# A filter table loaded earlier, a weight converted by its transfers, and finer steps beside the first two chunks of a fused FFT mixing and MLP kernel

## The chip, the cores and the metric

The kernel runs on one core of a Trainium2 chip. The metric is the device time of one execution in microseconds (us); lower is better. Of the engines, PE is the matrix engine (TensorE; PEld its weight loads), DVE the vector engine, ACT the scalar engine, POOL GpSimd and SP the engine that only issues transfers. Each engine works through its own instructions in order and waits where one of them is not ready. Transfers (DMA) run on 16 engines that all queues share; POOL and SP feed two different queues of them.

## The reference

```python
# x: 8 x 3008 x 256; filt_r, filt_i: 1505 x 256
X = rfft(x, axis=1)
y = irfft(X * (filt_r + 1j * filt_i)[None], n=3008, axis=1)
t = y.reshape(24064, 256)
# w_in: 256 x 2048, w_out: 2048 x 256, alpha: 2048
h = t @ w_in
s = sin(alpha * h)
out = (h + s * s / (alpha + 1e-9)) @ w_out
```

All inputs and the output are fp32. The kernel computes in fp16 with fp32 sums.

## The kernel before, in words

**The transform.** The length 3008 is split into 47 x 64. For one batch of 3008 rows, a first stage (`f1`, or `f1_chip` for batch 0) multiplies by a table of roots of order 47 (`wa`), a second (`f2x`) by `wb`, which gives the spectrum in `xs`; `product` multiplies it by the filter `fri` on DVE into `z` and `t2`; `f2g` (batch 0: `g_chip`) goes back by `wg` (and `wgs`), and `f3` by `we` into `yt`, which is the MLP's input. Between the stages the data must change its layout. Batches 1 to 7 do that through DRAM: `asb` is stored to `scr1` and read back as `bint` (`shuffle1`), `gsb` is stored to `scr2` and read back as `gin` (`shuffle2`); all of these go through SP's queue. Batch 0 does it on the chip, by multiplications with an identity: `turn1` ahead of `f2x`, `turn2` ahead of `f3`.

**The MLP.** The 24,064 rows are worked in 47 chunks `g` of 512 rows, each in 8 slots `q`. `mlp_in` multiplies by a block of `w_in16` and ACT takes the sine into `vt`; after every odd slot DVE squares four blocks (`square`); `mlp_out` of the chunk before multiplies `vt` by `w_out2` (`w_out` divided by `alpha`), and `yt` by `m_t`, the product of `w_in` and `w_out`, so that `h` itself is never kept. `evict_out` copies the sums `po` to `ot` on DVE, and `store_out` stores them by SP.

**The order.** Nothing schedules itself: the order in the program is the order on each engine. The part up to the first chunk is a written list. After that a dictionary `plan` says which work stands in which slot: `at(slot, f, ...)` puts it between the two `mlp_in` of that slot, and the loop calls it there. For batch 1, `f1` is put three to a slot from slot 5 on, `shuffle1` in slot 10, and the second stage from slot 14 on. Slots 0 to 13 (chunk 0, which has no `mlp_out` beside it, and most of chunk 1) also hold what is left over from the start: `turn2` 4 to 15, `prep_w_inT` (a transposed `w_in` for `m_t`), `prep_w_out` (`w_out2`), `prep_m` in slot 13, and `negate_filter`.

**Banks.** The matrix engine writes to eight banks: three `psf` (transform stages and preparations), three `psh` (`mlp_in`, `turn1`, `keep_busy`, half of `g_chip`) and two `pso` (`po` of `mlp_out`; before that, half of `g_chip`). A tile of a pool waits until the tile that had its bank has been evicted by ACT or DVE.

**Transfers at the start.** POOL issues `x` of batch 0 in four parts of two transfers each, then the filter in three parts (each of `filt_r` and `filt_i`, each in two transfers), then `w_in16`, all converted from fp32 to fp16 by the transfer. SP issues the tables; `gate(a, b)` makes the issue of transfer `a` wait until `b` has landed. The first third of `wb` goes at once; the rest waits for the first filter transfer, and the three slices of `wg` and `wgs` follow. `w_out` comes as fp32, its first half by SP behind a gate on `w_in16`, the second by POOL in slot 7; POOL converts each half to `w_out16` (`cast_w_out`). `load_x(1, 4)` brings batch 1's rows by POOL in eight transfers; it can start only when `f2x` of batch 0 is done with `bint`, whose memory it takes. `keep_busy` multiplies zeros, to no use but PE's clock.

Of the kernel before, what the change touches and what calls it, by code (L numbers as in the profile page):

```python
# [10 lines left out]
FP32 = mybir.dt.float32  # L11
# [53 lines left out]
def kernel(  # L65
# [57 lines left out]
    def gate(ins, earlier):  # L123

        tc.add_manual_dep(ins.ins, earlier.ins.name, mybir.DependencyInfo(
            mybir.DependencyClass.Sync, mybir.DependencyReason.DATA), reason="order of transfers")

    def load_x(b, parts=2):

        xt[b] = (xbpool if b else vpool).tile([GT, RP, C], FP16, name="xt", tag="xb" if b else "vt")  # L130
        n = RP // parts
        for h in range(parts):
            for p0, p1 in ((0, 80), (80, GT)):
                x_dma[b, h] = nc.gpsimd.dma_start(  # L134
                    out=xt[b][p0:p1, n * h:n * h + n, :],
                    in_=dram(x, (b * S + RP * p0 + n * h) * C, [[RP * C, p1 - p0], [1, n * C]]))
# [45 lines left out]

    def turn2(j):

        ps = psf.tile([4 * NK, 2, C], FP32, name="pst2", tag="f")
        rows = b_c.rearrange("p h r s a -> p h r (s a)")
        for i in range(2):
            for half in range(2):
                nc.tensor.matmul(out=ps[:, i, 128 * half:128 * half + 128],
                                 lhsT=rows[:, half, 2 * j + i], rhs=ident, start=True, stop=True)  # L190
        (nc.scalar.copy if j in (0, 2, 12, 14) else nc.vector.tensor_copy)(  # L191
            out=gin[0][:, 2 * j:2 * j + 2, :], in_=ps)

    def shuffle1(b):
# [88 lines left out]
    def mlp_out(g, q, h):  # L283

        if q == h:
            po[g, h] = pso.tile([128, 2, C], FP32, name="po", tag="po")
        if not 0 <= q - h < 7:
            return
        for n in range((q - h) * 36 // 7, (q - h + 1) * 36 // 7):
            k, i = divmod(n, 2)  # L290
            t = 2 * h + i
            ts = slice(128 * t, 128 * t + 128)
            nc.tensor.matmul(out=po[g, h][:, i, :],  # L293
                             lhsT=vt[g][:, k, ts] if k < 16 else yt[g][:, k - 16, t],
                             rhs=w_out2[:, k, :] if k < 16 else m_t[:, k - 16, :],
                             start=(n == 0), stop=(n == 35))
# [38 lines left out]
    alpha_r = cpool.tile([16, 128], FP32, name="alpha_r")  # L335
    alpha_t = cpool.tile([128, 16], FP32, name="alpha_t")
    recip = cpool.tile([128, 16], FP32, name="recip")
    w_inT, w_out32, w_in32, alpha_b = [], [], [], []

    def prep_alpha():  # L340
        ps = pso.tile([128, 2, C], FP32, name="psal", tag="po")
# [2 lines left out]
        nc.vector.tensor_scalar(out=recip, in0=alpha_t, scalar1=1e-9, scalar2=None, op0=ALU.add)  # L344
        nc.vector.reciprocal(out=recip, in_=recip)

    def load_w_out(h, eng):
        w_out32.append(stpool.tile([128, 8, C], FP32, name="w_out32", tag="st"))
        return eng.dma_start(out=w_out32[h],
                             in_=moe_w_out[1024 * h:1024 * h + 1024, :].rearrange("(b p) c -> p b c", p=128))  # L350

    def cast_w_out(h):
        nc.gpsimd.tensor_copy(out=w_out16[:, 8 * h:8 * h + 8, :], in_=w_out32[h])

    def prep_w_out(h, k):
        for i in range(4 * k, 4 * k + 4):
            nc.vector.tensor_scalar(out=w_out2[:, 8 * h + i, :], in0=w_out32[h][:, i, :],
                                    scalar1=recip[:, 8 * h + i:8 * h + i + 1], scalar2=None,
                                    op0=ALU.mult)

    def prep_w_inT(k):
        if k == 0:
            w_inT.append(ginpool.tile([128, 16, C], FP16, name="w_inT", tag="gin"))
        ps = psf.tile([128, 2, C], FP32, name="pst", tag="f")
        for i in range(2):
            for cb in range(2):
                jb = 2 * k + i
                nc.tensor.matmul(out=ps[:, i, 128 * cb:128 * cb + 128],
                                 lhsT=w_in16[:, cb, 128 * jb:128 * jb + 128],
                                 rhs=ident, start=True, stop=True)  # L370
        (nc.scalar.copy if k % 2 else nc.vector.tensor_copy)(
            out=w_inT[0][:, 2 * k:2 * k + 2, :], in_=ps)
# [45 lines left out]
    plan = {}  # L418

    def at(slot, f, *args):  # L420
        plan.setdefault(int(slot), []).append((f, args))

    for b in range(1, B):
        p = MT * (b - 1)
        u0, un, x0, step = (5, 3, 14, 1.1) if b == 1 else (p - 9, 2, p + 4, 1.9)
        for u in range(16):
            at(u0 + u // un, f1, b, u)
        at(u0 + 16 // un, shuffle1, b)
        for k in range(6):
            xa, xb = x0 + int(2 * k * step), x0 + int((2 * k + 1) * step)  # L430
            at(xa, f2x, b, 2 * k)
            at(xb, f2x, b, 2 * k + 1)
            at(xb + 1, product, b, k, 0)
            at(xb + 2, product, b, k, 1)
            at(xb + 4, f2g, b, 2 * k)
            at(xb + 5, f2g, b, 2 * k + 1)
        at(xb + 6, shuffle2, b)
        if b + 1 < B:
            at(xb + 1, load_x, b + 1)
    G = 2  # L440
    for g in range(NCH - 1):
        todo = []
        while G < 8 * B and GT * G < 128 * (g + 2):
            todo += [(G, 0), (G, 1)]
            G += 1
        slots = (4, 6) if len(todo) == 2 else (3, 4, 6, 7) if g == 4 else (3, 4, 5, 6)
        for q, u in zip(slots, todo):
            at(8 * g + q, f3, *u)
    for k in range(2):
        at(6 + k, prep_w_out, 0, k)  # L450
        at(10 + k, prep_w_out, 1, k)
        at(13, prep_m, k)
    at(6, cast_w_out, 0)
    at(7, load_w_out, 1, nc.gpsimd)
    at(10, cast_w_out, 1)
    at(14, load_w_in32, 0)
    at(22, load_w_in32, 1)
    for k in range(8):
        at(5 + k, prep_w_inT, k)
        at(18 + k + 3 * (k // 4), prep_w_ina, k // 4, k % 4)  # L460

    for k in range(3):
        at(11 + k, negate_filter, 8 * k, 8)
    for j in range(4, 16):
        at((j - 4) * 5 // 12, turn2, j)

    with tc.manual_schedule():
        nc.sync.dma_start(out=wa2, in_=wa2_d.ap())
# [18 lines left out]
                w_in_dma[h, cb] = nc.gpsimd.dma_start(out=w_in16[:, cb, hs],  # L487
                                                      in_=moe_w_in[128 * cb:128 * cb + 128, hs])
        wgs = ginpool.tile([128, NK * 128], FP16, name="wgs", tag="gin")
        gate(nc.sync.dma_start(out=wb[:, 8 * 128:], in_=wb_d.ap()[:, 8 * 128:]), filter_dma[0, 0])  # L490
        for s0 in (0, 8, 16):
            cs = slice(128 * s0, 128 * s0 + 1024)
            ins = nc.sync.dma_start(out=wg[:, cs], in_=wg_d.ap()[:, cs])
            if s0:
                gate(ins, filter_dma[s0, 0])
            nc.sync.dma_start(out=wgs[:, cs], in_=wgs_d.ap()[:, cs])
        a_c = vpool.tile([128, 2, NK, 128], FP16, name="a_c", tag="vt")
        prep_alpha()
# [7 lines left out]
        for f, *args in (  # L506
                (turn1, 0), (turn1, 1), (turn1, 2), (f2x, 0, 0), (turn1, 3), (turn1, 4), (f2x, 0, 1),
                (turn1, 5), (turn1, 6), (f2x, 0, 2), (turn1, 7), (fold_filter, 0, 8), (turn1, 8),
                (f2x, 0, 3), (product, 0, 0, 0), (turn1, 9), (f2x, 0, 4), (turn1, 10), (f2x, 0, 5),
                (product, 0, 1, 0), (turn1, 11), (keep_busy, 2, zero), (f2x, 0, 6), (f2x, 0, 7), (g_chip, 0, 0), (g_chip, 0, 1),  # L510
                (fold_filter, 8, 8), (f2x, 0, 8), (keep_busy, 2, zero), (product, 0, 2, 0), (g_chip, 1, 0), (g_chip, 1, 1),
                (f2x, 0, 9), (keep_busy, 2, zero), (product, 0, 3, 0), (f2x, 0, 10), (f2x, 0, 11), (keep_busy, 2, zero), (g_chip, 2, 0), (g_chip, 2, 1),
                (fold_filter, 16, 8), (keep_busy, 2, zero), (product, 0, 4, 0), (g_chip, 3, 0), (g_chip, 3, 1),
                (product, 0, 5, 0), (keep_busy, 2, zero), (g_chip, 4, 0), (g_chip, 4, 1), (keep_busy, 2, zero), (g_chip, 5, 0), (g_chip, 5, 1),
                (keep_busy, 1, zero)):
            f(*args)
        gin[0] = ginpool.tile([4 * NK, RP, C], FP16, name="gin", tag="gin")
        for j in range(4):
            turn2(j)
        gate(load_w_out(0, nc.sync), w_in_dma[0, 1])  # L520
        load_x(1, 4)
        for i in range(4):
            if i % 2 == 0:
                keep_busy(1, zero)
            f3(i // 2, i % 2)

        for g in range(NCH):
            for q in range(8):
                if g and q == 7:
                    evict_out(g - 1, 0)  # L530
                mlp_in(g, 2 * q)
                if g:
                    mlp_out(g - 1, q, 1)
                for f, args in plan.get(8 * g + q, ()):
                    f(*args)
                mlp_in(g, 2 * q + 1)
                if g:
                    mlp_out(g - 1, q, 0)
                if g and q == 7:
                    evict_out(g - 1, 1)  # L540
                    store_out(g - 1, 0, 4, (nc.sync,))
                if q % 2:
                    square(g, q)
# [29 lines left out]
```

## Time and profile before

| | |
|---|---|
| three runs, median | 836.46 us (836.37 to 837.84) |
| the profiled execution, its own time | 836.65 us |
| its span, first to last instruction | 834.9 us |
| busy: PE | 815.2 us (98%), 6242 matmuls |
| busy: ACT, DVE, POOL | 619.4, 513.4, 37.5 us |
| mean granted PE clock | 0.998 |
| first `mlp_in`; `prep_m`; first `mlp_in` of chunk 4 | 38.0, 70.7, 115.3 us |

Times in the profile are us from the start of the span. "Busy" is the time in which an engine has an instruction at work, and matmuls overlap: the distance between two starts says what a matmul really takes. A line such as `PE a L204 <- DMA b: 3.6, 1, 3.6` says that PE stood idle before line 204 of the kernel for 3.6 us in total, once, 3.6 at the longest, until the transfer of `b` had landed.

### The profile page before, as it was taken

What the parts mean: (1) busy time and instruction counts of PE and PEld (TensorE: products, weight loads), DVE (VectorE), ACT (ScalarE), POOL (GpSimd) and SP (SyncE); (2) the same over time, 40 slices, a digit from 0 to 9 for tenths busy, and PEclk for the clock granted to TensorE, in tenths of its full rate; (3) what the DMA queues carried; (4) which work ended last, traced back from release to release, by engine and by line L of the source; (5) the groups of instructions that cost most, each with busy time, mean ns of one, the idle gap of its engine ahead of it and who ended that gap; (6) DMA issues with size and microseconds to landing.
All of it is one profiled execution on the core that took longest, in us unless ns stands there. A gap on an engine that the chain in (4) does not pass through costs nothing.

```text
span 834.9 us, 15135 instructions
## 1 busy us (share of the span) xinstructions
PE 815.2 (98%) x6242; PEld 572.4 (69%) x6242; DVE 513.4 (61%) x676; ACT 619.4 (74%) x1155; POOL 37.5 (4%) x66
## 2 busy tenths in 40 slices
PE   6979999999999999999999999999999999999997
PEld 3647676777667776677767776677766777767666
DVE  4788966676466665576655684567655675443442
ACT  4786987787777877788777887778877787666663
POOL 6211000000000000000000000000000000000000
PEclk9999999999999999999999999999999999999999
DMA  9926383424543163612834146331645123210111
GB/s 196 246 85 244 105 205 84 144 73 113 139 110 119 51 162 89 202 40 65 193 95 139 51 110 168 102 101 51 168 110 150 53 101 92 62 51 26 26 52 51
DMA packets 67061, 92.33 MB, mean 111 GB/s; under 512 B 5512, under 2 KB 51352, under 8 KB 65480
## 3 DMA queue, kind: packets, MB, share of 16 engines
q1 hardware_dynamic: 60704, 72.04, 30.1%
q0 software_dynamic: 5760, 19.14, 11.0%
q8 instruction: 49, 0.80, 0.4%
q10 hardware_dynamic: 528, 0.18, 0.1%
q14 instruction: 20, 0.16, 0.1%
HBM read 59.62 MB, written 46.66 MB: 127 GB/s over the span
## 4 chain that ended last, share of the span: by engine, by line
PE 91%; DVE 3%; DMA 3%; issue 2%; POOL 0%; ACT 0%; POOLq 0%
PE po L293 42%; PE ph L274 37%; PE psa L143 2%; PE psy L262 2%; PE psx L204 2%; PE psg L234 2%; DMA w_out<-in_moe_w_out_dram 1%; PE pe L307 1%; DMA wb<-wb_tbl 1%; DMA xt<-in_x_dram 1%; PE psg L177 1%; DVE vt L281 1%; DVE gin L191 1%; DMA fri<-in_filt_r_dram 0%; PE idle L397 0%
## 5 line engine op out<-in xcount | busy, mean ns | idle before, releaser
L276 ACT ACTIVATE vt<-ph 128x512 f16<-128x512 f32 x688 | 404.8, 602 | 142.1 <-PE ph L274 137.2
L293 PE MATMUL po<-w_out,vt 128*128 128x256 f16 x2944 | 426.6, 272 | 1.3 <-DVE ot L318 0.8
L293 PEld LDWEIGHTS <-vt 128*128 128x128 f16 x2944 | 287.4, 98 | 173.1 <-issue 2.0
L274 PE MATMUL ph<-yt,w_ina 128*128 128x512 f16 x1376 | 399.3, 379 | 0.0
L281 DVE TENSOR_TENSOR vt<-vt 128x2048 f16<-128x2048 f16 x188 | 230.2, 1224 | 195.8 <-ACT vt L276 194.9
L274 PEld LDWEIGHTS <-w_ina 128*128 128x128 f16 x1376 | 128.2, 98 | 32.8
L318 DVE COPY ot<-po 128x512 f32<-128x512 f32 x92 | 63.0, 688 | 22.4 <-PE po L293 21.3
L208 ACT CAST xs<-psx 128x512 f16<-128x512 f32 x96 | 56.6, 593 | 10.8 <-PE psx L204 10.7
L144 DVE CAST asb<-psa 96x512 f16<-96x512 f32 x56 | 38.2, 685 | 33.4 <-PE psa L143 30.6
L236 ACT CAST gsb<-psg 128x512 f16<-128x512 f32 x84 | 49.5, 589 | 12.2 <-PE psg L234 11.2
L293 PE MATMUL po<-m_t,yt 128*128 128x256 f16 x368 | 55.2, 273 | 0.0
L267 DVE CAST yt<-psy 128x240 f16<-128x240 f32 (+45 forms) x92 | 32.2, 351 | 33.0 <-ACT yt L264 32.0
L264 ACT CAST yt<-psy 128x376 f16<-128x376 f32 (+46 forms) x127 | 45.9, 362 | 7.9 <-PE psy L262 1.0
L276 ACT ACTIVATE vt<-ph,alpha_t 128x512 f16<-128x512 f32 x64 | 42.8, 694 | 10.9 <-PE ph L274 10.1
L134 POOL DMA_DIRECT2D xt<-in_x_dram x40 | 21.4, 542 | 494.3 <-PE psy L262 287.4
L262 PE MATMUL psy<-we,gin 96*128 96x94 f16 x512 | 42.1, 204 | 0.7 <-ACT asb L144 0.7
L204 PE MATMUL psx<-bint,wb 128*128 128x256 f16 x192 | 37.2, 278 | 3.8 <-DMA wb<-wb_tbl 3.6
L262 PEld LDWEIGHTS <-gin 96*128 96x128 f16 x512 | 35.6, 97 | 7.6 <-issue 1.3
L293 PEld LDWEIGHTS <-yt 128*128 128x128 f16 x368 | 36.0, 98 | 4.2
L144 ACT CAST asb<-psa 96x512 f16<-96x512 f32 x56 | 32.3, 583 | 8.0 <-PE psa L143 7.7
L217 DVE TENSOR_TENSOR z<-xs,fri 128x1024 f16<-128x1024 f16 x48 | 33.0, 687 | 8.0 <-ACT xs L208 4.6
L274 PE MATMUL ph<-yt,w_in 128*128 128x512 f16 x128 | 36.4, 379 | 0.2 <-ACT yt L264 0.2
(70 smaller groups left out, 383.3 us busy)
## 6 DMA issues: line engine op xcount, KB each, us to landing
scr<-asb SPq DMA_DIRECT2D x14, 768.0 KB
bint<-scr SPq DMA_DIRECT2D x21, 512.0 KB
scr<-gsb SPq DMA_DIRECT2D x21, 512.0 KB
out_dram<-ot SPq DMA_DIRECT2D x31, 320.0 KB
xt<-in_x_dram POOLq DMA_DIRECT2D x12, 640.0 KB, 7.6
gin<-scr SPq DMA_DIRECT2D x7, 768.0 KB
out_dram<-ot SPq DMA_DIRECT2D x16, 256.0 KB
gin<-scr SPq DMA_DIRECT2D x7, 576.0 KB
```

The source lines that it names most:

```text
L144: (nc.vector.tensor_copy if u % 2 else nc.scalar.copy)(out=asb[b][:, 2 * u:2 * u + 2, :], in_=ps)
L204: nc.tensor.matmul(out=ps[:, i, :], lhsT=wb[:, 128 * (2 * t + i):128 * (2 * t + i) + 128], rhs=bint[b][:, 2 * t + i, :], start=True, stop= ...
L208: nc.scalar.copy(out=xs[b, t // 2][:, t % 2 * 2:t % 2 * 2 + 2, :], in_=ps)
L217: nc.vector.tensor_tensor(out=z[k], in0=xs[b, k], in1=fri[:, 0, k4, :], op=ALU.mult)
L236: nc.scalar.copy(out=gsb[b][:, 2 * t:2 * t + 2, :], in_=ps)
L262: nc.tensor.matmul(out=ps[:, t, :], lhsT=gin[b][:, 4 * a + t, 128 * cb:128 * cb + 128], rhs=we if b else we2, start=True, stop=True)
L264: (nc.vector.tensor_copy if G == 0 and cb else nc.scalar.copy)(out=yt[g][:, cb, :, lo:lo + n], in_=ps[:, :, 0:n])
L274: nc.tensor.matmul(out=ph, lhsT=(w_in16 if g < 4 else w_ina)[:, cb, 128 * jb:128 * jb + 128], rhs=yt[g][:, cb], start=(cb == 0), stop=(cb ...
L276: nc.scalar.activation(out=vt[g][:, jb, :], in_=ph, func=AFT.Sin, scale=alpha_t[:, jb:jb + 1] if g < 4 else 1.0)
L281: nc.vector.tensor_tensor(out=v4, in0=v4, in1=v4, op=ALU.mult)
L293: nc.tensor.matmul(out=po[g, h][:, i, :], lhsT=vt[g][:, k, ts] if k < 16 else yt[g][:, k - 16, t], rhs=w_out2[:, k, :] if k < 16 else m_t[ ...
L318: nc.vector.tensor_copy(out=ot[g][:, 2 * h:2 * h + 2, :], in_=po[g, h])
```

## The change

- The second part of `wb` is gated on the third quarter of `x` instead of the first filter transfer; the first slice of `wg` gets the gate on that filter transfer.
- `w_out` is loaded by two POOL transfers that convert to fp16, straight behind `load_x(1, 4)`; the fp32 buffers, POOL's conversions and the gate go away. `prep_w_out` reads the fp16 copy, four blocks each in slots 6, 8, 10 and 12 (before: 6, 7, 10, 11).
- `plan` has half steps: a second place in each slot, behind the slot's second `mlp_in` and `mlp_out`. What is planned for a whole slot stands where it stood.
- `f1` of batch 1 stands one in each half step from slot 4 to 11.5; `shuffle1` is in slot 12, and the second stage starts in slot 16 instead of 14, with all that follows it for batch 1.
- `turn2` 4 to 15 come in slots 0 to 3.5 instead of 0 to 4 and use the `pso` banks; ACT evicts 0, 2, 7, 10 and 13 (before: 0, 2, 12, 14). `prep_w_inT` moves half a slot later, and its first three use `pso`.
- In the written list `f2x` 7 of batch 0 stands behind the first `g_chip` pair instead of in front of it, and one `keep_busy` moves behind `f2x` 6.

```diff
@@ turn2
-        ps = psf.tile([4 * NK, 2, C], FP32, name="pst2", tag="f")
+        ps = (psf if j < 4 else pso).tile([4 * NK, 2, C], FP32, name="pst2", tag="f" if j < 4 else "po")
...
-        (nc.scalar.copy if j in (0, 2, 12, 14) else nc.vector.tensor_copy)(
+        (nc.scalar.copy if j in (0, 2) or j > 4 and j % 3 == 1 else nc.vector.tensor_copy)(
             out=gin[0][:, 2 * j:2 * j + 2, :], in_=ps)
@@ w_out
-    def load_w_out(h, eng):
-        w_out32.append(stpool.tile([128, 8, C], FP32, name="w_out32", tag="st"))
-        return eng.dma_start(out=w_out32[h],
-                             in_=moe_w_out[1024 * h:1024 * h + 1024, :].rearrange("(b p) c -> p b c", p=128))
-
-    def cast_w_out(h):
-        nc.gpsimd.tensor_copy(out=w_out16[:, 8 * h:8 * h + 8, :], in_=w_out32[h])
-
-    def prep_w_out(h, k):
+    def load_w_out(h):
+        return nc.gpsimd.dma_start(out=w_out16[:, 8 * h:8 * h + 8, :],
+                                   in_=moe_w_out[1024 * h:1024 * h + 1024, :].rearrange("(b p) c -> p b c", p=128))
+
+    def prep_w_out(k):
         for i in range(4 * k, 4 * k + 4):
-            nc.vector.tensor_scalar(out=w_out2[:, 8 * h + i, :], in0=w_out32[h][:, i, :],
-                                    scalar1=recip[:, 8 * h + i:8 * h + i + 1], scalar2=None,
-                                    op0=ALU.mult)
+            nc.vector.tensor_scalar(out=w_out2[:, i, :], in0=w_out16[:, i, :],
+                                    scalar1=recip[:, i:i + 1], scalar2=None, op0=ALU.mult)
@@ prep_w_inT
-        ps = psf.tile([128, 2, C], FP32, name="pst", tag="f")
+        ps = (pso if k < 3 else psf).tile([128, 2, C], FP32, name="pst", tag="po" if k < 3 else "f")
@@ plan
-        plan.setdefault(int(slot), []).append((f, args))
+        plan.setdefault(int(2 * slot), []).append((f, args))
...
-        u0, un, x0, step = (5, 3, 14, 1.1) if b == 1 else (p - 9, 2, p + 4, 1.9)
+        u0, x0, step = (4, 16, 1.1) if b == 1 else (p - 9, p + 4, 1.9)
         for u in range(16):
-            at(u0 + u // un, f1, b, u)
-        at(u0 + 16 // un, shuffle1, b)
+            at(u0 + u / 2 if b == 1 else u0 + u // 2, f1, b, u)
+        at(u0 + 8, shuffle1, b)
...
+    for k in range(4):
+        at(6 + 2 * k, prep_w_out, k)
     for k in range(2):
-        at(6 + k, prep_w_out, 0, k)
-        at(10 + k, prep_w_out, 1, k)
         at(13, prep_m, k)
-    at(6, cast_w_out, 0)
-    at(7, load_w_out, 1, nc.gpsimd)
-    at(10, cast_w_out, 1)
...
-        at(5 + k, prep_w_inT, k)
+        at(5.5 + k, prep_w_inT, k)
...
-        at((j - 4) * 5 // 12, turn2, j)
+        at((j - 4) / 3, turn2, j)
@@ transfers at the start
-        gate(nc.sync.dma_start(out=wb[:, 8 * 128:], in_=wb_d.ap()[:, 8 * 128:]), filter_dma[0, 0])
+        gate(nc.sync.dma_start(out=wb[:, 8 * 128:], in_=wb_d.ap()[:, 8 * 128:]), x_dma[0, 2])
         for s0 in (0, 8, 16):
             cs = slice(128 * s0, 128 * s0 + 1024)
-            ins = nc.sync.dma_start(out=wg[:, cs], in_=wg_d.ap()[:, cs])
-            if s0:
-                gate(ins, filter_dma[s0, 0])
+            gate(nc.sync.dma_start(out=wg[:, cs], in_=wg_d.ap()[:, cs]), filter_dma[s0, 0])
             nc.sync.dma_start(out=wgs[:, cs], in_=wgs_d.ap()[:, cs])
@@ the list
-                (product, 0, 1, 0), (turn1, 11), (keep_busy, 2, zero), (f2x, 0, 6), (f2x, 0, 7), (g_chip, 0, 0), (g_chip, 0, 1),
+                (product, 0, 1, 0), (turn1, 11), (f2x, 0, 6), (keep_busy, 2, zero), (g_chip, 0, 0), (g_chip, 0, 1), (f2x, 0, 7),
...
-        gate(load_w_out(0, nc.sync), w_in_dma[0, 1])
         load_x(1, 4)
+        load_w_out(0)
+        load_w_out(1)
@@ the loop over slots
-                for f, args in plan.get(8 * g + q, ()):
+                for f, args in plan.get(16 * g + 2 * q, ()):
                     f(*args)
                 mlp_in(g, 2 * q + 1)
                 if g:
                     mlp_out(g - 1, q, 0)
+                for f, args in plan.get(16 * g + 2 * q + 1, ()):
+                    f(*args)
```

More of the change, by code (lines that the diff above doesn't have):

```diff
@@ L337 @@
     recip = cpool.tile([128, 16], FP32, name="recip")
-    w_inT, w_out32, w_in32, alpha_b = [], [], [], []
+    w_inT, w_in32, alpha_b = [], [], []
     def prep_alpha():
```

## The prediction

> **What bounds the kernel now.** I read the busy time by stretches first. The columns are, after the stretch: its length, busy time (instructions) of PE, PEld, DVE, ACT and POOL, the granted PE clock, the DMA share and GB/s.
>
> ```profile
> 18.00:22.00 4.00, 0.42 (x6) 0.25 (x5) 3.87 (x6) 1.84 (x4) 0.80 (x2) 1.00 1.10 292
> 22.00:25.00 3.00, 3.00 (x17) 2.03 (x17) 1.43 (x2) 2.05 (x4) 0.00 (x0) 0.50 1.17 281
> 25.00:30.00 5.00, 5.00 (x62) 4.13 (x61) 3.30 (x5) 4.97 (x11) 0.46 (x1) 0.96 1.11 245
> 30.00:38.00 8.00, 7.27 (x95) 5.42 (x93) 5.55 (x10) 5.62 (x13) 4.24 (x8) 1.00 0.98 247
> 38.00:55.40 17.40, 13.99 (x110) 8.18 (x110) 15.88 (x30) 14.15 (x26) 2.57 (x1) 1.00 0.24 49
> 55.40:70.70 15.30, 13.90 (x113) 9.51 (x112) 12.39 (x20) 11.85 (x20) 2.86 (x2) 1.00 0.65 181
> 70.70:115.30 44.60, 43.77 (x344) 32.10 (x341) 39.73 (x58) 36.64 (x67) 3.87 (x7) 1.00 0.59 186
> 115.30:834.90 719.60, 714.87 (x5385) 502.62 (x5383) 423.89 (x535) 533.99 (x999) 10.35 (x20) 1.00 0.37 100
> ```
>
> From 115.3 us PE is full except in its last few us, and the diff leaves that part's instructions and order as they are. So the end moves by just what PE's idle or half-clocked time before 115 changes. DMA is full up to 42 us (share about 1.0).
>
> The waits up to 40 us give the first hole: PE stands 3.6 us before `psx` for the second part of `wb`. Behind it the clock is 0.50 for about three us.
>
> ```profile
> PE psx L204 <- DMA wb<-wb_tbl: 3.6, 1, 3.6
> ```
>
> The second hole is scattered, so I took PE's timeline from 38 us on, columns start, length, instruction, idle before it:
>
> ```profile
> 48.83 1.03 PE L274 MATMUL ph<-yt,w_in 128*128 128x512 f16 x4
> 49.69 0.81 PE L143 MATMUL psa<-xt,wa 94*96 94x512 f16 x3
> 51.24 0.33 PE L262 MATMUL psy<-we,gin 96*128 96x94 f16 x4 [0.74 <-ACT asb L144]
> 52.05 0.38 PE L368 MATMUL pst<-ident,w_in 128*128 128x128 f16 x4 [0.49 <-DVE asb L144]
> 52.27 1.03 PE L274 MATMUL ph<-yt,w_in 128*128 128x512 f16 x4
> ```
>
> Starts count here, since ends are modelled: four 512-column matmuls take 49.69 - 48.83 = 0.86, so 0.215 each; three `f1` are 0.65 and ended at 50.34, yet PE goes on at 51.24. That is 0.90 lost, because three `f1` in a row fill the three `psf` banks and the fourth tile waits for an eviction. The same sum over all starts from 38.0 to 70.7 gives 6.75 us lost: 17.4 us for chunk 0 (55.39 - 38.00) hold about 12.5 of PE work, and 1.9 is lost up to `prep_m` at 70.67. A last 0.99 is lost at 99.34, where PE waits for `ot` on DVE.
>
> The chain that ended last puts 8.46 us on the POOL load of `w_out` at 56.09. That is the load's length and not a loss: it hangs on DVE's `prep_w_out`, for which PE waited once, 0.43 at 66.70.
>
> **A. The start (`wb` sooner).** The old gate opened at 13.97; the new one is the third quarter of `x`, for whose rows PE waited until 10.87. So `wb` issues 3.1 us sooner. From issue to release it took 21.89 - 13.97 = 7.9 now; with the same, it lands at 18.8. PE stands there from 18.16, so the wait falls from 3.6 to about 0.6 and the clock stays up. The bytes go ahead of other traffic: between 17 and 21 SP's queue moved about 0.22 MB/us and POOL's about 0.07, against 0.19 alone. But `wb`, issued at 13.97, moved no packet before 16.9. With that 2.9 it starts at 13.8, behind the last quarter of `x` (12.79), and slows the filter instead. The filter's first two transfers then land near 16.7; `fold_filter` takes them at 18.39, so 1.7 us cover this.
>
> The Trainium skill, "DMA: Bandwidth & Descriptors", section "Queues, rings and completion order", says that each DMA engine takes turns between queues, packet by packet. By that `wb` would get turns at once and push the last quarter of `x` back, an estimated 0.5 off this term; the trace disagrees for the 2.9 us in which POOL's queue held all of the time.
>
> What is late next: the first `g_chip` needs the product (ready at 21.0 on DVE) and the first `wg`/`wgs` slices behind `wb`. I put it at 21.6 instead of 25.2. Then DVE is the chain: the second fold ends at 23.5, and four products of 1.21 (0.60 per instruction at its pitch) and the third fold of 1.2 make 6.05; the last `g_chip` starts at 29.7 instead of 33.28, 3.6 us sooner. Before that comes the third `wg` slice. It issued at 23.80, and its 2 KB packets ran from 27.0 to 30.5; block 4, which needs it, ran at 31.92. If it lands no sooner, block 4 starts at 30.5, the last 1.36 later at 31.9, 1.4 gained; 0.8 later than now, 0.6. But its gate, the third filter transfer, should open 1 to 1.6 us sooner, because SP's queue idles less between 10.9 and 17. I take **2.6** (ends 0.6 and 3.6). Moving `f2x` 7 behind block 0 and swapping `keep_busy` cost nothing: its product is due 3 us later. From there to 38.0 (`turn2` 0 to 3, first `f3`) nothing changes.
>
> **B. Chunks 0 and 1.** `turn2` 4 to 15 go to the two idle `pso` banks, spread over slots 0 to 3.5, nine on DVE instead of ten (0.61 each at the pitch). With two squares (1.13), DVE needs 7.75 for slots 0 to 3, and two banks hold PE to it: slot 4 starts at about 45.6 against 44.97 now, a loss of 0.6, but with `turn2` 14 and 15 done. Slots 4 to 7 then hold eight `f1`, one per half step: ACT has eight `Sin` (0.58), four `f1` (0.48), one `w_inT` (0.48), two `f3` (0.28), 7.6; DVE four `f1` and two `w_inT` (0.61), two squares, four `w_out2` rows, two `yt`, 7.4; PE 6.2. PE runs some 0.3 ahead of ACT's last items and reaches slot 8 at about 52.9 instead of 55.39: **2.5**. If DVE is not kept ahead by the banks, 1.0.
> From slot 8 to `prep_m` PE has 13.3 us of work now and gets one `f1` more (0.22), with enough room on ACT (11.4) and DVE (12.1); allow 0.3 of stalls: 13.8 instead of 15.28, **1.5** (ends 0.5 and 1.9).
> `w_out`: POOL loses two casts (2.57, 1.90), and DVE one row of 2.07 that ran beside the second cast; PE's 0.43 is in the sum above. The two POOL issues (0.96 each) follow `load_x(1)` on POOL's queue, with nothing behind them until slot 14. `x(1)` had all landed by 42, with `w_out` on SP beside it; at 0.19 MB/us two halves of 0.52 MB take 5.5, so they land by 45 and 48 at the latest, while `prep_w_out` 0 and 2 come at about 49 and 57, or 46.6 and 54.4 when A is taken off (then `x(1)` starts sooner too). `w_out2` from half-width rows costs DVE 0.27 a row as now, or less (the 2048-column `negate_filter` took 0.61); I keep 0.27. The last four rows come in the slot that uses the first of them; DVE reaches it about 0.3 us ahead of PE, else 0.5.
>
> **C. Batch 1, two slots later.** `shuffle1` stays four slots ahead of its first `f2x`; now the loads issue at 68.84 and PE takes them at 76.12. DVE's products still overlap `prep_w_ina`: 15.1 us of work in 14.3 of PE time in slots 18 to 23, against 19.0 in 18.6 in slots 16 to 23 now. So the 0.99 stall stays: **0** (ends -0.7 and +0.8). SP: the `asb` stores and `shuffle1` keep their order, and the `gsb` stores change places with output stores only. The last `f2g` comes five slots before the first `f3` of batch 1 instead of seven, some 10.5 us. Now it ran at 114.69, `gin` issued at 119.08 and its first rows had moved by about 122, 7 us: covered by 3. POOL's `load_x(2)` comes at slot 29 and takes 8.4; `f1` reads it at slot 38.
>
> **Sum.** 2.6 + 2.5 + 1.5 + 0 = 6.6. The profiled run took 836.65 (span 834.9, 1.75 around it), 0.19 above the median of 836.46. So 836.65 - 6.6 = **830.0**.
>
> **Rivals.**
> 1. The start gives little (0.6), because the third `wg` slice, and behind it DMA, sets block 4: for it DMA's full share until 42; against it the idle of SP's queue before 16.9. 830.05 + 2.0 = 832.1.
> 2. Chunk 0 stays bound by evictions: ACT and DVE hold 14.15 and 15.88 of 17.4 us, and `turn2` has two banks. B gives 1.5: 832.5 with part A, 835.2 at the low ends of all three.
> 3. All of it: A 3.6, C 0.8, and B 5.2, if ACT's 13.7 us of work alone set chunk 0 (17.4 - 13.7 = 3.7) and nothing is lost after: 9.6, so 827.0.
> 4. Slower: `w_out` lands late. `prep_w_out` then stands at the head of DVE's queue with evictions and squares behind it, and PE stops when the `psf` banks are full. With `x(1)` in at 42 and h per half, the second half lands at 42 + 2h, due at 54.4. The 6.6 are used up at 61, h = 9.5; at 12.5, as the half issued on SP took, it lands at 67, 12.6 late: 830.05 + 12.6 = 842.6. For it: that row, and POOL's queue had 4.7% of DMA from 32 to 34 beside `w_out`'s packets on SP's. Against: the half issued on POOL took 8.46, of which its packets moved from 59 to 63.6 only, behind an `asb` store; and DMA stands idle from 44 to 54.
>
> The Trainium skill, "SBUF — State Buffer", section "SBUF: two separate sides", warns that vector instructions in a two-port mode keep POOL from writing descriptors, and advises the other queues, which speaks for this rival. The eight `load_x(1)` issues took 4.70 beside a DVE fold of 1.22, against 4.27 for the first eight, so the trace shows 0.4 us at most.
>
> 5. The change does nothing that PE sees: `wb` lands as late as now behind the filter, and `turn2`'s two banks take back what the half steps give: 836.6.
>
> **Chances.** Forecast 0.56, rival 1 0.17, rival 2 0.11, rival 3 0.07, rival 4 0.06, rival 5 0.03. Faster than 0.2% (1.7 us, about what a measurement here tells from no change) are the first four, less 0.02 of rival 2's low end: 0.89; same 0.05; slower 0.06. The range takes in rivals 1 and 3 and most of 2, and leaves out 4 and 5: 826.6 to 834.4.
>
> **What would show it.** The wait on `wb` under 1 us and no 0.50 clock at 22 to 25; last `g_chip` at about 30.7; first `mlp_in` at 35.4; `prep_m` near 64, with gaps before `psy` and `w_inT` under 0.3; chunk 4's first `mlp_in` near 108.7; PE full after that. A wait on `w_out` in DVE's queue, on `wg` in PE's, or on `gin` at the first `f3` of batch 1 would prove it wrong, as would idle PE after 110.

## The result, and the profile after

The changed kernel takes 834.65 us (median of 20 runs, 832.60 to 836.87) against 836.73 (20 runs, 836.22 to 838.82): the ratio is 0.9974, with a 95% interval of 0.9966 to 0.9983. That is 2.1 us faster, where 6.6 were forecast. The profiled execution is the longest of the 20: 836.87, with a span of 835.0. What its profile says of the start is therefore the bad end, and the median is 2.2 us better.

First, as before, busy time by stretches (length, then PE, PEld, DVE, ACT and POOL, the granted PE clock, the DMA share and GB/s):

```profile
18.00:22.00 4.00, 2.65 (x27) 1.66 (x24) 3.18 (x5) 4.00 (x10) 1.76 (x2) 1.00 1.19 239
22.00:25.00 3.00, 1.87 (x18) 1.82 (x18) 2.29 (x4) 1.21 (x3) 1.96 (x3) 0.71 1.14 185
25.00:30.00 5.00, 4.35 (x33) 2.80 (x32) 3.75 (x6) 4.11 (x8) 1.03 (x2) 0.83 1.03 214
30.00:38.00 8.00, 4.57 (x62) 3.74 (x62) 2.81 (x5) 3.22 (x6) 5.28 (x10) 1.00 1.08 238
38.00:55.40 17.40, 15.90 (x146) 9.96 (x144) 14.26 (x22) 13.96 (x26) 0.49 (x1) 1.00 0.57 81
55.40:70.70 15.30, 14.44 (x113) 9.52 (x111) 13.66 (x32) 13.46 (x26) 0.00 (x0) 1.00 0.31 81
70.70:115.30 44.60, 44.10 (x347) 32.40 (x345) 37.72 (x54) 36.87 (x66) 3.87 (x7) 1.00 0.56 181
115.30:834.90 719.60, 715.39 (x5390) 503.01 (x5387) 425.14 (x538) 534.26 (x1000) 10.30 (x20) 1.00 0.38 101
```

The first row shows the gain that was meant: from 18 to 22 PE has 27 matmuls instead of 6. Behind it the gain is lost again: from 22 to 25 PE has 18, hardly more than the 17 of before, and in the two stretches from 25 to 38 it has 33 and 62 where there were 62 and 95. The clock was 0.71 from 22 to 25 and 0.83 from 25 to 30 (0.50 and 0.96 before): the time at half clock came later and did not go away, for from 23.2 to 26.5 the granted clock was 0.51. The two stretches with the half steps are fuller (15.90 instead of 13.99, 14.44 instead of 13.90).

The waits up to 140 us say what took the place of the 3.6 us on `wb`:

```profile
PE psg L177 <- DMA wgs<-wgs_tbl: 4.8, 3, 1.9
PE psg L177 <- DMA wg<-wg_tbl: 1.4, 2, 1.0
DVE fri L407 <- DMA fri<-in_filt_i_dram: 1.4, 2, 0.7
PE psx L204 <- DMA wb<-wb_tbl: 0.2, 1, 0.2
```

The wait on `wb` is gone, as forecast (under 1). In its place PE waits 6.2 us in `g_chip` for the tables that come behind `wb`, and DVE 1.4 for the filter, which it never waited for before. The chain that ended last (start, length, what) names the two transfers in the start that carry this:

```profile
14.44 10.77 DMA fri<-in_filt_r_dram
25.60 10.61 DMA wgs<-wgs_tbl
36.24 1.00 PE psg L177 x15
```

A filter transfer issued at 14.44 lands 10.8 us later; only then does the last `wgs` slice issue, which again takes 10.6; then PE goes on at 36.24.

PE's timeline, for the second hole (start, length, instruction, idle before):

```profile
50.68 0.38 PE L143 MATMUL psa<-xt,wa 94*96 94x512 f16 x1
50.90 0.33 PE L262 MATMUL psy<-we,gin 96*128 96x94 f16 x4
51.07 0.60 PE L274 MATMUL ph<-yt,w_in 128*128 128x512 f16 x2
51.51 0.38 PE L143 MATMUL psa<-xt,wa 94*96 94x512 f16 x1
70.03 0.27 PE L293 MATMUL po<-w_out,vt 128*128 128x256 f16 x1 [0.59 <-DVE w_out L353]
```

One `f1` now stands between other work, and the starts follow without a gap (0.22, 0.17, 0.44); the 0.74 and 0.49 of before are gone. One wait above 0.3 us is left ahead of `prep_m`: 0.59 for the last rows of `w_out2`.

So the part up to chunk 4 splits into three stretches. Marks in the profiled executions, in us: the first two columns are times from the start of the span, the next two the time from the mark before.

| | last `g_chip` block | first `mlp_in` | to `prep_m` | to chunk 4 | own time |
|---|---|---|---|---|---|
| before | 33.28 | 38.00 | 32.67 | 44.67 | 836.65 |
| after | 37.51 | 42.23 | 29.28 | 43.90 | 836.87 |
| gates_back | 32.78 | 37.51 | 29.27 | 43.92 | 832.14 |
| slices_free | 34.27 | 38.99 | 29.28 | 43.83 | 833.52 |
| wb_split | 34.09 | 38.81 | 29.28 | 43.83 | 833.87 |
| wb_lastx | 33.89 | 38.62 | 29.28 | 43.83 | 833.18 |
| wb_thirds | 32.90 | 37.62 | 29.28 | 43.84 | 832.71 |
| w_in_late | 32.03 | 36.76 | 29.26 | 43.83 | 831.29 |
| both_late | 32.59 | 37.31 | 29.28 | 43.84 | 831.85 |
| gates_only | 40.31 | 46.08 | 32.92 | 44.66 | 844.98 |
| w_out_only | 34.33 | 39.05 | 31.81 | 44.66 | 836.39 |
| w_out_back | 32.79 | 37.52 | 36.24 | 44.68 | 840.38 |

Wherever the half steps and the converted `w_out` are both in, the second stretch is 29.26 to 29.28 us and the third 43.83 to 43.92. From there to the end of the span it is 719.5 us, or 720.0 in wb_split, wb_thirds and w_out_back and 719.1 in w_out_only. So nearly all that varies among the versions with both lies ahead of the first `mlp_in`.

The start must be read with care, since each version has one profile. Those of after and gates_only are of their slowest runs; those of w_in_late, both_late, wb_split and w_out_back are of their fastest. And w_out_only, which changes nothing ahead of 29 us, reached its first `mlp_in` 1.05 us later than before: a difference of that size between two profiles shows nothing.

### The profile page after: what moved, and what is told of

Read it like the earlier page. It is cut to its first block, busy times and chain, and to the rows that moved or that the text cites. A ratio compares the mean times of both kernels' runs of the same rounds, so it can differ in the third digit from the quotient of the medians.

```text
span 835.0 us, 15131 instructions
## 1 busy us (share of the span) xinstructions
PE 816.3 (98%) x6242; PEld 573.1 (69%) x6242; DVE 509.9 (61%) x675; ACT 619.0 (74%) x1156; POOL 35.0 (4%) x65
## 4 chain that ended last, share of the span: by engine, by line
PE 91%; DMA 3%; DVE 3%; ACT 1%; POOL 1%; issue 0%; SPq 0%; POOLq 0%; DVEq 0%
PE po L293 42%; PE ph L274 37%; PE psa L143 3%; PE psy L262 3%; PE psg L234 2%; PE psx L204 2%; DMA fri<-in_filt_r_dram 1%; DMA wgs<-wgs_tbl 1%; PE pe L307 1%; DMA xt<-in_x_dram 1%; DVE vt L281 1%; PE psm L372 0%; ACT vt L276 0%; DVE gin L191 0%; DVE w_ina L385 0%
## 5 line engine op out<-in xcount | busy, mean ns | idle before, releaser
L318 DVE COPY ot<-po 128x512 f32<-128x512 f32 x92 | 62.9, 688 | 22.2 <-PE po L293 21.3
L236 ACT CAST gsb<-psg 128x512 f16<-128x512 f32 x84 | 49.5, 589 | 11.5 <-PE psg L234 10.7
L134 POOL DMA_DIRECT2D xt<-in_x_dram x40 | 21.3, 540 | 491.8 <-PE psy L262 300.7
```

The source lines that it names most:

```text
L236: nc.scalar.copy(out=gsb[b][:, 2 * t:2 * t + 2, :], in_=ps)
L318: nc.vector.tensor_copy(out=ot[g][:, 2 * h:2 * h + 2, :], in_=po[g, h])
```

## The experiments

The question is where the start's 2.6 us went. **Theory 1**: the bytes of `wb` go ahead of the filter; the filter's later transfers land later, and with them the gates of the second and third `wg`/`wgs` slices open later. **Its rival**: the start is as forecast or nearly so, and the missing time lies in the half steps or in `w_out`. Each round of runs had the kernel before beside it, at medians of 837.45, 837.17 or 836.75 us, and the ratios are to those runs.

**The start's two gate lines undone (gates_back), and done alone (gates_only).**

```diff
 gates_back, against after
-gate(dma(wb, second part), x_dma[0, 2])
+gate(dma(wb, second part), filter_dma[0, 0])
-    gate(dma(wg, slice s0), filter_dma[s0, 0])
+    ins = dma(wg, slice s0)
+    if s0:
+        gate(ins, filter_dma[s0, 0])
 gates_only, against before: the same lines the other way round, and nothing else
```

> The changed kernel with the two gates of the start as they were before (wb behind the first filter transfer, first wg slice without a gate); all else stays changed. Theory 1 (wb in front of the filter holds the filter back, and through their gates the second and third wg/wgs slices): the 4.2 us lost before the first mlp_in go away, it stands at 38.0 again, the wait on wb is back at 3.6, and the gains after it (3.4 to prep_m, 0.8 to chunk 4) stay: 832.4 beside 836.7 of the kernel before. Theory 2 (the loss at the start comes from what else was moved there: f2x 7 behind the first g_chip pair, or w_out on POOL's queue): first mlp_in still near 42, 834.6.

> The kernel before with the two gates of the changed kernel and nothing else. Theory 1: it loses what the changed kernel lost at the start, 2 us in the middle and 4.2 in the run that was profiled, so 838.7 to 841, with waits of PE on wgs of 3 to 5 us and none on wb. Theory 2: the wait on wb goes and nothing takes its place: 833.5 to 834.

Measured: gates_back 832.67 (832.02 to 833.48), ratio to before 0.9943 (0.9926 to 0.9959); gates_only 839.87 (836.80 to 844.98), ratio 1.0035 (1.0016 to 1.0054). The two lines cost 2.0 us with the rest of the change by the bare medians (834.65 less 832.67, from two rounds) and some 2.6 by the two ratios to before (0.9974 and 0.9943), and 2.4 without it (839.87 less 837.45, which before took beside it). Both times lie where theory 1 put them or within 0.3 us of it, and neither is near theory 2's. The waits of PE, the first line of gates_back and the second of gates_only:

```profile
PE psx L204 <- DMA wb<-wb_tbl: 2.6, 1, 2.6
```

```profile
PE psg L177 <- DMA wgs<-wgs_tbl: 6.6, 3, 3.9
```

With the old gates the old wait on `wb` is back, and it costs less than what the new gates bring. SP's issues show the gates, `wb` first and then the second and third `wg` slices (start, length, queue, what); after first, then before:

```profile
10.83 0.32 SPq L482 DMA_DIRECT2D wb<-wb_tbl  x1
22.44 0.32 SPq L485 DMA_DIRECT2D wg<-wg_tbl  x1
25.23 0.32 SPq L485 DMA_DIRECT2D wg<-wg_tbl  x1
```

```profile
13.97 0.32 SPq L490 DMA_DIRECT2D wb<-wb_tbl  x1
16.83 0.32 SPq L493 DMA_DIRECT2D wg<-wg_tbl  x1
23.80 0.32 SPq L493 DMA_DIRECT2D wg<-wg_tbl  x1
```

`wb` issues 3.1 us sooner, and the second slice issues 5.6 later and the third 1.4 later. For the second gate this is clear of the scatter: the three profiles with both new gate lines as they are (after, gates_only, w_in_late) have it at 22.1 to 22.4, the six with the old gates at 16.8 to 18.5. For the third it is less so: 25.2 to 25.8 against 22.7 to 25.1. Now POOL's issues (after, then before; idle before in brackets), first the filter transfer that opens the second gate:

```profile
12.15 0.58 POOL L401 DMA_DIRECT2D fri<-in_filt_r_dram  x1
17.11 0.49 POOL L397 DMA_DIRECT2D fri<-in_filt_i_dram  x1 [2.08 <-DMA fri<-in_filt_i_dram]
19.57 1.21 POOL L401 DMA_DIRECT2D fri<-in_filt_i_dram  x1 [1.96 <-DMA fri<-in_filt_i_dram]
20.76 0.56 POOL L479 DMA_DIRECT2D w_in<-in_moe_w_in_dram  x1
```

```profile
12.22 0.58 POOL L406 DMA_DIRECT2D fri<-in_filt_r_dram  x1
15.79 0.58 POOL L406 DMA_DIRECT2D fri<-in_filt_i_dram  x1 [0.37 <-DMA fri<-in_filt_i_dram]
16.46 1.82 POOL L487 DMA_DIRECT2D w_in<-in_moe_w_in_dram  x3
```

The transfer that opens the second gate issues no later than before, at 12.15 for 12.22, and so does the one for the third gate, at 14.44 for 14.35. They land late: 10.3 us after the issue instead of 4.6, and 10.8 instead of 9.5. From 12 to 17 us SP's queue moved 0.51 MB, where it had moved 0.01 before, and POOL's 0.69 instead of 0.95. By its bytes alone POOL's queue was some 2.2 us behind: the 0.91 MB that it had moved from 12 us to the opening of the old gate at 16.83 were reached at 19.0. Why the gate opened 3.4 us later still, at 22.44, is not shown.

The two waits of POOL come behind these issues and delay what follows. No line of the kernel asks for them: by the profile POOL stands before an issue until an earlier transfer of its queue has landed, 2.08 and 1.96 us, and everything behind it slides. The first issue of `w_in16` comes at 20.76 instead of 16.46, 4.3 us later.

**Whether the harm grows with the bytes of `wb` and with their place (slices_free, wb_split, wb_lastx).** All three against after:

```diff
 slices_free
-    gate(dma(wg, slice s0), filter_dma[s0, 0])
+    gate(dma(wg, slice s0), filter_dma[0, 0])
 wb_split: only the middle third goes early
-gate(dma(wb[8:]), x_dma[0, 2])
+gate(dma(wb[8:16]), x_dma[0, 2])
+gate(dma(wb[16:]), filter_dma[0, 0])
 wb_lastx
-gate(dma(wb[8:]), x_dma[0, 2])
+gate(dma(wb[8:]), x_dma[0, 3])
```

> The changed kernel, but the second and third wg slices wait for the first filter transfer only, so that all tables follow each other on SP's queue. Theory 1a (the late gates are how wb's bytes do harm: the second opened at 22.4 instead of 16.8): the waits on wg/wgs fall from 6.2 to 2 us or less, first mlp_in at 36 to 39, 829.5 to 832.5. Theory 1b (it is the order of the bytes on a full DMA, gates or not): the filter is late instead, DVE's folds wait, first mlp_in at 40 or later, 833.5 or more.

> The changed kernel, but only the middle third of wb (256 KB) waits for the third quarter of x; the last third waits for the first filter transfer, ahead of wg. Theory 1, the bytes of wb in front of the filter do the harm in proportion: the second wg gate opens at 19 to 20 (16.8 before, 22.4 in the changed kernel), first mlp_in at 38 to 40, 832 to 834. Rival (the filter is held whenever SP's queue has any bytes before it): gate at 22 or later, first mlp_in at 41 or later, 835.

> The changed kernel with wb behind the last quarter of x, some 1.2 us sooner than before instead of 3.1. Theory 1: part of the harm, gate of the second slice at 18 to 21, first mlp_in at 38 to 41, 832.5 to 834.5. Rival: as harmful as the changed kernel, 835 or more.

Measured: slices_free 833.24 (831.18 to 834.59), ratio 0.9946 (0.9927 to 0.9964); wb_split 834.11 (833.87 to 834.85), 0.9964 (0.9952 to 0.9976); wb_lastx 833.64 (832.89 to 836.27), 0.9962 (0.9950 to 0.9974). With half of the bytes, or with all of them 2.1 us later, the second gate opens at 18.3 instead of 22.4, and the first `mlp_in` comes at 38.6 to 38.8. That is far from after and rules out both rivals. But it is within what the old gates show too (16.8 to 18.5, and 37.3 to 39.1). So it is shown that fewer bytes, or later ones, open the second gate sooner; a harm in proportion to them is not shown. With the later slices no longer gated on the later filter transfers (slices_free), PE's waits for `wg` and `wgs` fall from 6.2 to 2.4, but the filter is late instead. This is DVE's wait there:

```profile
DVE fri L407 <- DMA fri<-in_filt_i_dram: 4.1, 3, 2.3
```

The first `mlp_in`, at 38.99, is at the end of theory 1a's range, and the time lies between 1a's range and 1b's. So the late gates were a large part of the loss, since without them slices_free comes close to gates_back (0.9946 and 0.9943); and the bytes of `wb` still do harm by another way, since the filter now comes late. From 10 to 38 us the transfers share one full resource, and what goes ahead is paid by what comes behind. The times of these three versions can't be told apart by their intervals; their profiles show different waits.

**Only a third of `wb` behind the first `wg` slice (wb_thirds).** Against gates_back:

```diff
-gate(dma(wb[8:]), filter_dma[0, 0])
+gate(dma(wb[8:16]), filter_dma[0, 0])
 dma(wg, slice 0); dma(wgs, slice 0)
+dma(wb[16:])
```

> The gates as before and all else as changed, but the second part of wb is cut in two, and its last third goes behind the first wg and wgs slices, so that nothing goes ahead of the filter. Theory 1: the wait for the middle third falls from 2.6 to 1 or less without any harm to the filter, the first g_chip comes about 1.5 us sooner, first mlp_in at 36 to 37, 830.5 to 832. Rival: the straggling of SP's packets sets the landing and not their number, wait on wb unchanged, 832.7.

Measured: 832.88 (832.45 to 833.72), ratio 0.9948 (0.9937 to 0.9960): no gain over gates_back. PE's timeline:

```profile
20.37 0.39 PE L204 MATMUL psx<-bint,wb 128*128 128x256 f16 x2 [1.69 <-DMA wb<-wb_tbl]
31.63 0.22 PE L177 MATMUL psg<-wgs,t 128*128 128x128 f16 x1 [1.12 <-DMA wgs<-wgs_tbl]
```

The wait on `wb` did fall, by 0.9 (from 2.6), but the block that needs the third `wgs` slice waits 1.12 where it waited 0.31 in gates_back, 0.8 more: the table behind is late by nearly what the table ahead has gained. Theory 1's wait (1 or less) and its time (830.5 to 832) are both missed. The wait did move: in the profiles with all of `wb` behind the old gate it is 2.4 to 4.1.

**What holds the last slices (w_in_late, both_late).** In after the last `wgs` slice needs 10.6 us from issue to landing. DMA packets by queue (q1 takes SP's transfers, q0 POOL's; packets, MB, share), in after from 35 to 36 us:

```profile
q0 software_dynamic: 75, 0.20, 100.8%
q1 hardware_dynamic: 3, 0.00, 1.3%
```

POOL's queue, with `w_in16` and batch 1's `x`, holds all of the time, and SP's queue, where the slice that PE waits for is the last transfer, gets three packets in a microsecond. The edit is the same for both, against after and against gates_back:

```diff
 dma(wgs, last slice)
+gate(first dma of w_in16 on POOL, dma(wgs, last slice))
```

> The changed kernel with one edit: the first transfer of w_in16 on POOL waits until the last slice of wgs has landed, and with it all that follows it on POOL's queue (the rest of w_in16, x of batch 1, w_out). Theory 1: in the changed kernel the last wg and wgs slices (issued at 25.2 and 25.6, needed until 36.2) are slow because w_in16 and x of batch 1 fill POOL's queue beside them. Without these the two slices (0.52 MB at some 0.19 MB/us, 2.8 us, and 2.3 to 3 until the first packet) land near 31, the waits on wgs fall from 4.8 to under 2, the last g_chip block starts at 32 to 33 instead of 37.5 and the first mlp_in at 37 to 38; the gates themselves stay late (second one near 22). What it can cost: w_in16 lands 6 us after 31, and w_out later still; 0 to 2 us. Time 831 to 833.5. Rival: it's the late gates alone, behind wb's bytes. Then the last slice still lands 10 us after its issue, w_in16 is not there before 42, and the time is 835.5 or more.

> The version with both gates of before (832.67, the best so far) with the same edit: w_in16 and all behind it on POOL's queue wait for the last wgs slice. There the last g_chip block started at 32.78 and waited for no table but wb (2.6). Theory 1 (POOL's bytes hold up SP's tables): the third slices have the queue to themselves, wb and the first slices are as they were, since w_in16 starts only behind the filter; the block that needs the third slice doesn't wait now, so nothing is gained: 832.3 to 833.5, with a loss of up to 1 us where w_in16 is late for the first mlp_in (37.5). Rival: w_in16's bytes also slow wb, which landed at 21.3 while w_in16 was on its way from 16.5; then the wait on wb falls from 2.6 to about 1.5 and the time to about 831.5.

Measured: w_in_late 833.12 (831.29 to 833.98), ratio 0.9950 (0.9937 to 0.9964); both_late 831.97 (831.85 to 833.19), ratio 0.9948 (0.9935 to 0.9962). From w_in_late, POOL's issue of `w_in16`, which shows when the last slice had landed, and PE's wait:

```profile
29.68 2.14 POOL L485 DMA_DIRECT2D w_in<-in_moe_w_in_dram  x4 [8.48 <-DMA wgs<-wgs_tbl]
```

```profile
PE psg L177 <- DMA wgs<-wgs_tbl: 1.3, 1, 1.3
```

The gates are as late as in after (22.35 and 25.51), but the last slice, issued at 25.89, lands by 29.68: 3.8 us instead of 10.6. The waits on `wgs` fall from 4.8 to 1.3, and the first `mlp_in` comes at 36.76 instead of 42.23. These two profiles are of the fastest run of one version and the slowest of the other, so their 5.5 us overstate it. By the medians the edit is worth 1.5 us (834.65 less 833.12), and 2.0 by the ratios to before. So theory 1 has to be put more exactly: a large part of the loss needs the late gates and, beside the last slices, POOL's later bytes, which slid there. Whether late gates alone would cost anything is not shown. In both_late the wait on `wb` doesn't fall (3.4), so the rival's 1.5 is out; the third slice's 0.31 goes, and by the time nothing that could be measured is gained, as theory 1 said. gates_back, w_in_late and both_late are not told apart in time. Each beats both kernels; against before it is by 4.2 to 4.8 us by their ratios.

**The steps without the converted `w_out` (w_out_back), and `w_out` alone (w_out_only).**

```diff
 w_out_back, against gates_back (and w_out_only, against before, the other way round)
-at(6 + 2 * k, prep_w_out, k)          # 4 blocks, from w_out16
-load_w_out(0); load_w_out(1)          # POOL, converting, behind load_x(1, 4)
+at(6 + k, prep_w_out, 0, k); at(10 + k, prep_w_out, 1, k)   # k < 2, from fp32
+gate(load_w_out(0, nc.sync), w_in_dma[0, 1])
+at(6, cast_w_out, 0); at(7, load_w_out, 1, nc.gpsimd); at(10, cast_w_out, 1)
```

> The kernel before with the half steps, the idle banks, f1 two a slot and the new place of f2x 7 alone: gates and w_out as before. Theory 1: within 0.7 us of gates_back on the slow side (DVE's wait for w_out beside POOL's cast comes back, 0.4 to 0.6 of PE): 832.5 to 833.2. Theory 2, if w_out on POOL's queue was what cost: faster than gates_back by 2 us or more, 830.5 or less.

> The kernel before with w_out converted by its transfers and prep_w_out in slots 6, 8, 10, 12, nothing else. Theory 3 (with the old steps the load of w_out hid behind chunk 0, and it becomes the bound only when the steps come sooner): PE's 0.43 and DVE's 2 us, so 0.3 to 1.0 faster, 836.2 beside 837. Rival: the conversion is worth its 7 to 8 us by itself, 830 or less.

Measured: w_out_back 841.11 (840.38 to 844.63), ratio 1.0049 (1.0030 to 1.0068), 8.4 us behind gates_back; w_out_only 835.16 (834.74 to 837.10), ratio 0.9977 (0.9967 to 0.9987). Both theories missed w_out_back by a wide margin. Its timelines of POOL, DVE and PE:

```profile
54.73 0.96 POOL L349 DMA_DIRECT2D w_out<-in_moe_w_out_dram  x1 [8.36 <-issue]
```

```profile
63.91 2.85 DVE L357 TENSOR_SCALAR w_out<-w_out,recip 128x256 f16<-128x256 f32 x4 [3.88 <-DMA w_out<-in_moe_w_out_dram]
```

```profile
66.03 1.01 PE L293 MATMUL po<-w_out,vt 128*128 128x256 f16 x4 [3.71 <-DVE w_out L357]
```

The second half of `w_out` can issue only in slot 7, at 54.73, and lands 9.2 us later. With the half steps, slot 10, whose rows of `w_out2` need it, comes before that: DVE is there at 60.03 and stands 3.88, and PE 3.71. Not all of PE's wait is the load: the load landed at 63.9, and the last 2.1 us are DVE's work on these rows. Beside POOL's conversion of the same half (63.94, 1.89 long) four rows take 2.85, where four took 1.13 at 53.02 and 67.28 without one. Behind that the clock is at half, as the busy time from 66 to 72 us shows (the columns are those of the stretches above):

```profile
66.00:72.00 6.00, 5.60 (x26) 3.25 (x26) 5.91 (x13) 1.61 (x3) 0.00 (x0) 0.50 0.19 50
```

With the wait and the half clock, the second stretch takes 36.24 us instead of 29.27, and the third 44.68 instead of 43.92. Without the half steps the same load is barely in time: DVE waited 0.6 for it in the profile of before. So the converted `w_out` is worth 0.86 us alone in the profiled stretch (31.81 instead of 32.67) and some 8 with the steps. The 2.0 us by the medians of w_out_only (837.17 less 835.16) are more than that stretch shows, and more than theory 3's 0.3 to 1.0; where the rest lies stays open.

## Why the prediction was right or wrong

**A, the start: forecast 2.6 (0.6 to 3.6) sooner, in the profile of after 4.2 later; this is the step that failed.** Its first part held: `wb` issued at 10.83, released PE 8.0 us later (7.9 was taken), the wait fell to 0.2, and the first `g_chip` started at 21.86 (21.6). From there on it failed. That block's second matmul came only at 23.21, after a wait of 1.13 for the first `wgs` slice, and the block then ran at half clock. Above all, the third slice's gate "should open 1 to 1.6 us sooner, because SP's queue idles less". It opened 1.4 later, and the second one, which had no term in the sum, 5.6 later. What `wb` did to the landing of the filter transfers that open these gates was taken for a gain. The 1.7 us of cover for `fold_filter` were counted for the first two filter transfers only. What the delay does to the transfers behind them on POOL's queue was not priced: the rest of the filter, then `w_in16`, which was through its issues at 21.3 before and at 25.3 after, and so lies beside the third slices. That is a large part of the cost: w_in_late, with the same late gates, starts the last block at 32.03 instead of 37.51 in its profile, and is 1.5 to 2.0 us faster in the median.

In the median the start is not quite so bad: if the other two stretches are as in the profile, 834.65 puts the first `mlp_in` near 40.0 (42.23 less the 2.2 between the profiled run and the median), 2.0 late instead of 2.6 early. That is 4.6 of the 4.65 by which 834.65 misses 830.0; that the 0.6 which B lacks and the 0.8 which C brings about cancel is luck. This split of the median is worked out from one profile and not measured.

The Trainium skill, "DMA: Bandwidth & Descriptors", section "Queues, rings and completion order", has each engine take turns between the queues packet by packet, which the prediction weighed as a 0.5 us delay for `x`. The bytes did push in: from 14 to 15 us SP's queue moved 0.31 MB and POOL's 0.02. But they fell on the filter, not on `x`: the last quarter of `x` released PE at 13.11, and the first packet of `wb` came at 13.28. And of the 2.9 us that the prediction held against turn-taking, some 0.9 pass before an SP transfer's first packet even when POOL's queue moves nothing. From 33 to 36 us SP's queue got 10 packets and POOL's 206, which looks like the opposite of taking turns. It need not be: the ten came one at a time, 0.1 to 0.4 us apart, as they would if one or two engines still had them to move and a POOL packet (0.17 or 0.32 us) ran in between. The trace does not name the engine, so this stays open. Where both queues had much to move, in gates_only from 36 to 41 us, they got 287 packets (SP) and 281 (POOL), which agrees with what the Trainium skill says.

**B, the half steps and `w_out`: forecast 4.0, measured 3.39 (32.67 to 29.28).** The mechanism held in each part. Slots 0 to 3 took 8.02 (7.6 forecast; two banks hold PE to DVE's copies, with gaps of 0.16 and 0.21). Slots 4 to 7 took 6.48 (7.3 forecast), so slot 8 is reached 14.50 after the first `mlp_in` instead of 14.9: 2.9 gained where 2.5 were forecast. From slot 8 to `prep_m` it is 14.78 against 15.28, 0.5 gained for 1.5: the low end. There the waits of 0.59 for the last rows of `w_out2` (priced 0.5 if DVE isn't ahead) and of 0.27 before an `f1` stand where 0.3 in all was allowed. Counted by starts, as the prediction counts, they are 0.74 and 0.44, and so nearly all of the 1.0 that is missing.

**`w_out`'s place in the sum was wrong, though its number did no harm.** The prediction said of the 8.46 on the chain that it "is the load's length and not a loss" and gave the conversion the 0.43 that PE waited. For before that is right. But the half steps come sooner to the rows that this load feeds, so it was the next thing to be late, and w_out_back puts that at 8 us. B came out only because both parts were in the change, and that is luck. Rival 4's mechanism (`w_out` late, DVE's queue held, PE standing) is much what w_out_back shows; in after the loads land in time and there is no such wait.

**C: forecast 0 (-0.7 to 0.8), measured 0.77 by the marks.** Two of batch 1's `f2g` groups now run behind chunk 4's mark (115.84 and 118.02; the last was at 114.69), which takes some 0.4 out of the stretch; what lies behind the mark is no longer for it, 719.55 us to the end of the span for 719.53. The other 0.3 is the wait for `ot`: 0.67 instead of 0.99 by starts (0.50 and 0.83 in the view). No `gin`, `wg` or idle PE shows behind 116: that cover held.

**Rivals.** Rival 1 named the right slice but had its end 0.8 later than now at most; the last block was 4.2 later (37.51 for 33.28). Rival 2 (B only 1.5) and rival 5 (nothing) are out by 3.39 and by the wait on `wb`. Rival 3 is out by the start.

**By the marks to look for**, the wait on `wb` was right; the clock (0.51 from 23.2 to 26.5), the last block (37.51 for 30.7), `prep_m` (71.51 for 64) and chunk 4 (115.41 for 108.7) were not. The one listed as proof against it, "on `wg` in PE's" queue, is what came.

## What to carry to other kernels

While the transfers are the full resource, a table that goes sooner is paid for by what stands behind it: follow every later transfer of every queue to its gate and to its user, not only the next one. If a gate is to help, let it hold back bytes that nobody needs yet (here `w_in16` and batch 1's `x`), rather than let needed bytes out sooner. With `wb` early this was worth 1.5 to 2.0 us; with the old gates it gained nothing that could be measured. And where steps become denser, price each load that is in time now by how much sooner it will be asked for; here a load with 0.6 us of wait came to cost some 8, with the slow rows and the half clock behind it.

## What the runs showed of the hardware that was not expected

- POOL's issue of a transfer stood 2.08 and 1.96 us, by the profile until an earlier one on its queue had landed, with no wait in the program.
- The first packet of an SP transfer came 0.9 us after its issue when POOL's queue moved nothing (issue 54.72, packet 55.59 in before), and 3.0 us after it when POOL's queue was full (13.97 and 16.94).
- Beside a full POOL queue an SP transfer of the same size took 10.6 us from issue to landing, and 3.8 with POOL's queue empty from 26 us on (w_in_late); SP's last packets came at 2 to 5 per us.
- The versions with the new gates scatter more: the 20 runs of after spread over 4.3 us, the 20 of before beside them over 2.6; the 12 of gates_only over 8.2, the 17 of before in that round over 4.5. Which packets make a run long or short was not traced.
